# Sixty-four more bytes in each x and h tile of two fused MLPs

## The chip, the core and the metric

The kernel runs on one core of a Trainium2 chip. The metric is the device time of one execution in microseconds; the kernel before was run three times, and the median counts. One further execution was taken by the hardware profiler, and every row below is from it.

## The reference, cut to what matters

The program is an attention with mixed heads, followed by two MLPs on its 1792 x 768 output:

```
scores = einsum(q @ k.T / 8, w_pre) over heads;  attn = softmax(scores)
x = (einsum(attn, w_post) over heads) @ v          # 1792 tokens x 768
h = x @ moe_w_in      (768 -> 2048);  h = elu(h);      x = h @ moe_w_out   (2048 -> 768)
h = x @ moe2_w_in     (768 -> 2048);  h = relu(h)**2;  out = h @ moe2_w_out (2048 -> 768)
```

Inputs and outputs are float32. The MLP weights arrive in float64 and are turned into float32 on the chip.

## The kernel before, in words

The attention comes first and takes about 430 us. The MLPs fill the rest, in two halves of 896 tokens. Everything in them that goes through TensorE is split into a high part (rounded to the type float32r) and a low part (the rest, also float32r). A product is made of three matmuls that add into one PSUM bank: high by high, high by low and low by high (`three`, L582 to L586).

In a matmul one operand is loaded into the array beforehand (the stationary one, by an LDWEIGHTS row, engine PEld) and the other is streamed through it (the moving one, row MATMUL, engine PE). The trace names a matmul as output<-moving,stationary. In three of the four layers the weights are stationary and the activations move, transposed, in pieces of 448 tokens (a float32r row of 1792 bytes per partition):

- first layer of the first MLP: `xh` and `xl` move past `wh` and `wl` (`inner`, L588)
- second layer of the first MLP: `hh` and `hl` move past `wh` and `wl` (loop at L645)
- first layer of the second MLP: `xh` and `xl` again (`inner`)
- second layer of the second MLP: here `hh` and `hl` are stationary, 128 tokens at a time, and `wh` and `wl` move in pieces of 384 columns (loop at L662)

With 16 blocks of 128 hidden units, 6 blocks of 128 model units, 2 pieces of 448 tokens and 2 halves, each of the lines L584, L585 and L586 runs 768 times with x moving and 384 times with h moving, that is 3456 matmuls of 448 columns in the three lines together. With wh and wl moving there are 16 x 2 x 7 x 2 = 448 per line, 1344 in all.

The order of the work is fixed by the order of the code on each engine. For every unit of weights (128 rows by 384 or 512 columns) SP starts a load, ScalarE and VectorE turn it into float32 and split it into `wh` and `wl` (`Weights`), two units ahead of its use. Between these, ScalarE and VectorE apply the activation to a finished bank and split the result into `hh` and `hl` (L617 to L626) or `xh` and `xl` (L655, L656).

The tiles `xh`, `xl`, `hh` and `hl` are made by `two_parts` (L524). A tile is 64 bytes longer than its content (`2 * OFF` floats with OFF = 8), and its content begins at float `at`: 8 for x, 0 for the h of the first MLP, 8 for the h of the second. Tiles of a pool lie one behind the other in each partition, the high one first. With the pools as they stand, the high parts begin, where they move, at a multiple of 128 bytes, and the low parts 64 bytes past one.

Of the kernel before, what the change touches and what calls it, by code (L numbers as in the profile page):

```python
# [8 lines left out]
F32R = mybir.dt.float32r  # L9
# [14 lines left out]
OFF = 8  # L24
# [481 lines left out]
class Mlps:  # L506
# [17 lines left out]
    def two_parts(self, k, pool, name, at):  # L524

        n = k * 2 * S
        t = [pool.tile([128, n + 2 * OFF], F32R, name=f"{name}{a}", tag=f"{name}{a}") for a in "hl"]
        return [x[:, at : at + n].rearrange("p (k s) -> p k s", k=k) for x in t]


# [199 lines left out]
```

## Time and profile before

| | us |
|---|---|
| median of 3 runs (lowest to highest) | 1381.85 (1380.25 to 1382.3) |
| profiled execution, time | 1380.11 |
| its span, first to last instruction | 1378.3 |
| TensorE matmuls busy in the span | 1366.5 (99%) |
| VectorE busy | 859.0 (62%) |
| ScalarE busy | 669.5 (49%) |
| GpSimd busy | 263.4 (19%) |

Matmuls are pipelined: a row's duration reaches from the start of a matmul to its modelled end, and the next one begins long before that. What a stream of matmuls costs is therefore read from the distance between the starts of two that follow each other, not from the durations. The granted clock of TensorE, a column of the windows below, is a share of 2.4 GHz, at which 448 columns take 186.7 ns and 384 columns 160.0 ns.

### The profile page before, as it was taken

The page shows a single profiled execution, that of the slowest core. Times are in us where ns is not written, and L with a number is a line of the kernel's source. Part 1 is how long each engine was busy: PE and PEld are TensorE (multiplying, and loading weights), DVE is VectorE, ACT ScalarE, POOL GpSimd, SP SyncE. Part 2 cuts the span into 40 slices and gives each one's busy share as a digit, 9 for nine tenths or more (in the row PEclk, how much of TensorE's full clock was granted, in tenths as well). Part 3 has the DMA queues.
Part 4 walks back from the last instruction along what each step waited for, and adds up shares of the span by engine and source line. Part 5 has one row for each costly group of instructions (what it writes and reads, how often), then busy time and mean ns, then how long its engine had stood idle before and what let it go on. Part 6 is the DMA issues. An engine that isn't in the chain of part 4 may idle for free.

```text
span 1378.3 us, 24196 instructions
## 1 busy us (share of the span) xinstructions
PE 1366.5 (99%) x8908; PEld 1247.3 (90%) x8908; DVE 859.0 (62%) x1928; ACT 669.5 (49%) x1504; POOL 263.4 (19%) x245
## 2 busy tenths in 40 slices
PE   7999999999999999999999999999999999999998
PEld 4888888888888999999999999999999999999998
DVE  6877778777886999866699996634442113443121
ACT  5776767776766667422355543235541113333111
POOL 3765655674656000000000000000000000000000
PEclk9999999999999999999999999999999999999999
DMA  5624633733644655545454576431121111111131
GB/s 155 203 106 134 197 106 126 210 119 114 201 139 129 200 167 175 185 156 171 128 164 158 173 251 194 156 103 58 54 77 54 47 46 46 58 52 58 41 109 40
DMA packets 104810, 174.40 MB, mean 127 GB/s; under 512 B 22675, under 2 KB 82163, under 8 KB 104691
## 3 DMA queue, kind: packets, MB, share of 16 engines
q1 hardware_dynamic: 104691, 172.85, 39.7%
q8 instruction: 70, 1.15, 0.3%
q14 instruction: 49, 0.40, 0.1%
HBM read 97.93 MB, written 36.18 MB: 97 GB/s over the span
## 4 chain that ended last, share of the span: by engine, by line
PE 97%; DVE 1%; ACT 0%; issue 0%; DMA 0%; POOL 0%; SPq 0%; ACTq 0%; DVEq 0%; POOLq 0%
PE ps_post L221 12%; PE ps_qk L585 11%; PE ps_qk L586 11%; PE ps_qk L584 11%; PE ps_qk L246 6%; PE ps_mix L585 6%; PE ps_post L585 6%; PE ps_post L586 6%; PE ps_mix L586 6%; PE ps_mix L584 6%; PE ps_post L584 6%; PE ps_qk L163 4%; PE ps_mix L192 3%; PE ps_mix L190 3%; PE ps_mix L191 3%
## 5 line engine op out<-in xcount | busy, mean ns | idle before, releaser
L472 ACT CAST wh<-wf 128x384 fp32r<-128x384 f32 (+1 forms) x240 | 126.7, 532 | 272.8 <-DVE wf L458 115.6
L473 DVE TENSOR_TENSOR wl<-wf,wh 128x384 fp32r<-128x384 f32 (+1 forms) x238 | 137.3, 580 | 158.2 <-ACT wh L472 157.2
L184 POOL TENSOR_TENSOR gl<-graw,gh 120x448 fp32r<-120x448 f32 x178 | 201.5, 1154 | 145.7 <-ACT gh L179 139.7
L221 PEld LDWEIGHTS ps_post<-wg,ex 120*112 120x112 f32 x1440 | 156.9, 177 | 20.6 <-DVE tot L205 7.5
L221 PE MATMUL ps_post<-wg,ex 120*112 120x120 f32 x1440 | 173.3, 273 | 0.0
L199 ACT ACTIVATE ex<-ps_mix,nmax 120x448 f32<-120x448 f32 x180 | 113.3, 636 | 113.0 <-DVE nmax L197 109.6
L585 PE MATMUL ps_qk<-xl,wh 128*128 128x448 f32 x384 | 141.0, 367 | 0.0
L586 PE MATMUL ps_qk<-xh,wl 128*128 128x448 f32 x384 | 140.6, 366 | 0.0
L584 PE MATMUL ps_qk<-xh,wh 128*128 128x448 f32 x384 | 139.4, 363 | 0.0
L197 DVE TENSOR_REDUCE nmax<-ps_mix 120x1 f32<-120x448 f32 x180 | 109.7, 622 | 41.8 <-PE ps_mix L192 41.4
L228 DVE COPY at<-ps_post 112x480 f32<-112x480 f32 x162 | 105.4, 650 | 10.0 <-PE ps_post L221 10.0
L179 ACT CAST gh<-graw 120x448 fp32r<-120x448 f32 x180 | 95.2, 593 | 0.6 <-DMA graw<-sc 0.5
L622 DVE TENSOR_TENSOR tmp<-tmp 128x448 f32<-128x448 f32 x64 | 39.9, 623 | 73.7 <-ACT tmp L621 73.7
L166 ACT COPY sc<-ps_qk 120x448 f32<-120x448 f32 x178 | 82.0, 557 | 7.2 <-PE ps_qk L163 7.0
L246 PEld LDWEIGHTS ps_qk<-at,v 112*64 112x64 f32 x1536 | 73.8, 137 | 11.3 <-ACT gh L179 6.2
L246 PE MATMUL ps_qk<-at,v 112*64 112x110 f32 (+2 forms) x1536 | 81.8, 262 | 0.0
L584 PEld LDWEIGHTS ps_qk<-xh,wh 128*128 128x128 f32 x384 | 72.3, 188 | 6.4
L585 PEld LDWEIGHTS ps_qk<-xl,wh 128*128 128x128 f32 x384 | 72.0, 187 | 6.3
L586 PEld LDWEIGHTS ps_qk<-xh,wl 128*128 128x128 f32 x384 | 72.0, 187 | 5.3
L434 ACT ACTIVATE wf<-wd 128x384 f32<-128x384 f32 (+1 forms) x120 | 69.5, 579 | 13.4 <-DMA wd<-w1i 7.9
L585 PE MATMUL ps_qk<-wl,hh 128*128 128x384 f32 x224 | 75.3, 336 | 0.0
L584 PE MATMUL ps_qk<-wh,hh 128*128 128x384 f32 x224 | 75.3, 336 | 0.0
(139 smaller groups left out, 3151.0 us busy)
## 6 DMA issues: line engine op xcount, KB each, us to landing
graw<-sc SPq DMA_DIRECT2D x180, 210.0 KB
wd<-w1i SPq DMA_DIRECT2D x32, 384.0 KB
wd<-w1o SPq DMA_DIRECT2D x24, 512.0 KB
wd<-w2i SPq DMA_DIRECT2D x32, 384.0 KB
wd<-w2o SPq DMA_DIRECT2D x32, 384.0 KB
w1if<-wf SPq DMA_DIRECT2D x32, 192.0 KB
w1of<-wf SPq DMA_DIRECT2D x24, 256.0 KB
w2if<-wf SPq DMA_DIRECT2D x32, 192.0 KB
```

The costliest lines, as they stand in the source:

```text
L179: nc.scalar.copy(hi, graw[t])
L184: engine.tensor_tensor(lo, graw.pop(t), parts[t][0].bitcast(F32), ALU.subtract)
L197: nc.vector.tensor_reduce(nmax, p, AX.X, ALU.max, negate=True)
L199: nc.scalar.activation(e[-1], p, AF.Exp, bias=nmax, scale=1.0, accum_out=tot[:, t % 2 : t % 2 + 1])
L221: nc.tensor.matmul(p[:, c, :], e[:, c * NJ : (c + 1) * NJ], w, start=True, stop=True)
L228: nc.vector.tensor_copy(o, p)
L246: nc.tensor.matmul(p[64 * a : 64 * a + 64, k, :w], vt[b, i][:, jc, g * D : (g + 1) * D], at[n][:, jc, 6 * i + g, :w], start=(jc == 0), sto ...
L472: nc.scalar.copy(hi, f)
L473: (engine or nc.vector).tensor_tensor(lo, f, hi.bitcast(F32), ALU.subtract)
L584: mm(p, wh, xh, start=first, stop=False)
L585: mm(p, wh, xl, start=False, stop=False)
L586: mm(p, wl, xh, start=False, stop=last)
```

## The change

Each tile of `two_parts` is given 128 bytes beyond its content, where it had 64:

```diff
     def two_parts(self, k, pool, name, at):
 
         n = k * 2 * S
-        t = [pool.tile([128, n + 2 * OFF], F32R, name=f"{name}{a}", tag=f"{name}{a}") for a in "hl"]
+        t = [pool.tile([128, n + 4 * OFF], F32R, name=f"{name}{a}", tag=f"{name}{a}") for a in "hl"]
         return [x[:, at : at + n].rearrange("p (k s) -> p k s", k=k) for x in t]
```

No instruction is added, removed or moved on any engine. What changes is where tiles lie in a partition. The contents are 21,504 bytes for x and 57,344 for h, both multiples of 128, as the pieces of 1792 bytes in them are. This is the first byte of the content, with its remainder by 128:

| content | before | after |
|---|---|---|
| xh, moving | 186,240 (0) | 186,112 (0) |
| xl, moving | 207,808 (64) | 207,744 (0) |
| hh of the first MLP, moving | 16,512 (0) | 16,512 (0) |
| hl of the first MLP, moving | 73,920 (64) | 73,984 (0) |
| hh of the second MLP, stationary | 16,544 (32) | 16,544 (32) |
| hl of the second MLP, stationary | 73,952 (96) | 74,016 (32) |
| wh, wl of three layers, stationary | (96) | 128 bytes lower (96) |
| wh, wl of the last layer, moving | (0) | 128 bytes lower (0) |

The pools of tmp, wd and wf lie 128 bytes lower too. The attention's tiles stay where they are; in its L190 to L192 the moving tiles gh and gl all begin at remainder 64.

## Rows read from the trace of the kernel before

**Rows 1.** The page: busy time of each engine; the chain that ended last, by engine.
```profile
PE 1366.5 (99%) x8908; PEld 1247.3 (90%) x8908; DVE 859.0 (62%) x1928; ACT 669.5 (49%) x1504; POOL 263.4 (19%) x245
...
PE 97%; DVE 1%; ACT 0%; issue 0%; DMA 0%; POOL 0%; SPq 0%; ACTq 0%; DVEq 0%; POOLq 0%
```

**Rows 2.** Groups by line, PE; names, tile, count | busy us, mean ns | idle us before.
```profile
L585 PE MATMUL ps_qk<-xl,wh 128*128 128x448 f32 x384 | 141.0, 367 | 0.0
L586 PE MATMUL ps_qk<-xh,wl 128*128 128x448 f32 x384 | 140.6, 366 | 0.0
L584 PE MATMUL ps_qk<-xh,wh 128*128 128x448 f32 x384 | 139.4, 363 | 0.0
...
L585 PE MATMUL ps_qk<-hl,wh 128*128 128x448 f32 x192 | 70.5, 367 | 0.0
```

**Rows 3.** Timeline, PE, 600 to 640: start us, duration us; first and last of 197.
```profile
599.81 0.37 PE L586 MATMUL ps_post<-hh,wl 128*128 128x448 f32 x1
...
639.66 0.36 PE L584 MATMUL ps_mix<-hh,wh 128*128 128x448 f32 x1
```

**Rows 4.** Timeline, PE, 1200 to 1240: first and last of 197 rows.
```profile
1199.83 0.37 PE L585 MATMUL ps_qk<-xl,wh 128*128 128x448 f32 x1
...
1239.68 0.37 PE L586 MATMUL ps_post<-xh,wl 128*128 128x448 f32 x1
```

**Rows 5.** Timeline, PE, 830 to 864: first and last of 197 rows.
```profile
829.69 0.34 PE L586 MATMUL ps_post<-wh,hl 128*128 128x384 f32 x1
...
863.66 0.34 PE L584 MATMUL ps_mix<-wh,hh 128*128 128x384 f32 x1
```

**Rows 6.** Timeline, PE, 500 to 501.3: seven matmuls in a row.
```profile
499.97 0.36 PE L584 MATMUL ps_post<-xh,wh 128*128 128x448 f32 x1
500.17 0.37 PE L585 MATMUL ps_post<-xl,wh 128*128 128x448 f32 x1
500.38 0.37 PE L586 MATMUL ps_post<-xh,wl 128*128 128x448 f32 x1
500.58 0.36 PE L584 MATMUL ps_post<-xh,wh 128*128 128x448 f32 x1
500.78 0.37 PE L585 MATMUL ps_post<-xl,wh 128*128 128x448 f32 x1
500.99 0.37 PE L586 MATMUL ps_post<-xh,wl 128*128 128x448 f32 x1
501.19 0.36 PE L584 MATMUL ps_mix<-xh,wh 128*128 128x448 f32 x1
```

**Rows 7.** Timeline, PE, 136.5 to 138: the attention's mixing matmuls, moving operands at 64.
```profile
136.71 0.36 PE L191 MATMUL ps_mix<-gh,pre_h 120*120 120x448 f32 x1
136.90 0.36 PE L192 MATMUL ps_mix<-gl,pre_h 120*120 120x448 f32 x1
137.10 0.36 PE L190 MATMUL ps_mix<-gh,pre_l 120*120 120x448 f32 x1
137.30 0.36 PE L191 MATMUL ps_mix<-gh,pre_h 120*120 120x448 f32 x1
137.50 0.37 PE L192 MATMUL ps_mix<-gl,pre_h 120*120 120x448 f32 x1
```

**Rows 8.** Timeline, PE, 93.9 to 95.3: first and last of five such matmuls.
```profile
94.05 0.36 PE L191 MATMUL ps_mix<-gh,pre_h 120*120 120x448 f32 x1
...
94.86 0.37 PE L192 MATMUL ps_mix<-gl,pre_h 120*120 120x448 f32 x1
```

**Rows 9.** Windows: from:to, us, busy (count) by engine, granted clock, DMA, GB/s.
```profile
450.00:550.00 100.00, 100.00 (x494) 92.30 (x493) 91.93 (x194) 68.72 (x138) 0.00 (x0) 1.00 0.56 179
560.00:660.00 100.00, 100.00 (x494) 92.30 (x493) 66.52 (x118) 30.16 (x53) 0.00 (x0) 1.00 0.51 162
800.00:890.00 90.00, 90.00 (x521) 90.00 (x520) 67.69 (x145) 31.85 (x65) 0.00 (x0) 1.00 0.64 205
1145.00:1245.00 100.00, 100.00 (x494) 92.30 (x493) 43.61 (x81) 38.58 (x82) 0.00 (x0) 1.00 0.18 53
```

**Rows 10.** Groups by line, VectorE, 430 to 1378: the writers of hl and xl.
```profile
L626 DVE TENSOR_TENSOR hl<-tmp,hh 128x448 fp32r<-128x448 f32 x128 | 74.1, 619 | 1.7 <-DMA xd<-xs 1.3
...
L656 DVE TENSOR_TENSOR xl<-ps_qk,xh 128x448 fp32r<-128x448 f32 x12 | 7.5, 624 | 40.3 <-ACT xh L655 40.3
```

## The prediction

> **What bounds the kernel now.** The first view to read is the page's busy line and its chain by engine [rows 1]: TensorE's matmuls are busy 99% of the span, and 97% of the chain that ended last is PE. So no wait of TensorE is to be removed, and a change counts if, and only if, it alters the rate at which matmuls follow one another. The second view, the groups by line, says that the matmuls of the MLPs sat idle for 0.0 us [rows 2]. Their durations there (363, 367 and 366 ns) overlap and are no cost; the column to read is the start, in the timeline.
>
> The timeline gives the rate. With h moving, the 197 rows from 599.81 to 639.66 make 196 steps of 39.85 / 196 = 203.3 ns [rows 3]. With x moving, in a late stage, it is again 39.85 / 196 = 203.3 ns [rows 4]. With the weights moving, in pieces of 384, it is 33.97 / 196 = 173.3 ns [rows 5]. The windows say what else goes on: VectorE is busy 92, 67 and 44 of 100 us and DMA 56, 51 and 18%, while TensorE starts the same 494 matmuls in each, at a granted clock of 1.00, the 2.4 GHz level [rows 9]. So the rate depends on no other engine and on no transfer; it is TensorE's own.
>
> At 2.4 GHz, 384 columns take 160.0 ns and 448 take 186.7. So a 384-column matmul costs 13.3 ns beyond its columns (173.3 - 160.0, 32 cycles), and a 448-column one 16.7 ns (203.3 - 186.7, 40 cycles). Both come each with one weight load of 128 columns. What differs, beside the length, is where the moving operands begin: all three of a group at a multiple of 128 bytes in the 384 case, and at 0, 64, 0 past one in the 448 case. The 3.3 ns between the two surpluses are what the change may win.
>
> **The change part by part.** (a) Nothing is issued more or less, and no queue is passed, so no instruction has to be priced; only places of tiles differ. (b) xl and hl move from remainder 64 to 0. They are one moving operand in three. The trace of before shows no 448-column stream with all three at 0, so its price is bounded. From below: the length may carry the 3.3 ns, and then it is 203.3 ns, nothing gained; an actual loss is the last rival. From above: the surplus of the aligned 384-column stream, 13.3 ns, as both load 128 weight columns per matmul; then it is 186.7 + 13.3 = 200.0 ns [rows 5]. Between the two lie the attention's mixing matmuls, 448 columns of the same type, all at remainder 64, with loads of 120 columns. Four steps there take 137.50 - 136.71 = 0.79 us in one place, 198 ns each [rows 7], and 94.86 - 94.05 = 0.81 us, 203 ns each, in another [rows 8]. A long row of 448 columns can thus run at about 200 ns when all its operands begin alike, which speaks against blaming the length. I take 200.0 ns, as the row nearest in type, weights and alignment is the 384-column one, and keep 203.3 for the range.
>
> The sum: 768 + 384 = 1152 matmuls in each of three lines, 3456 in all (the 384 rows of xl into ps_qk, two of four banks, are half of the 768 [rows 2]). 3456 x 3.33 ns = 11.5 us off 3456 x 203.3 ns = 703 us. The gain is not on xl's own matmul alone: the small differences inside a group (0.20 to 0.21 us from row to row [rows 6]) don't put it there, so the sum takes the whole group of three, 10 ns in 610.
>
> The Trainium skill has a rule that speaks against this. The profile shows 203.3 ns where the operands begin at 0, 64, 0 [rows 3]; the page SBUF — State Buffer, section "Door 1: The DMA port swizzle", says that consecutive accesses to one 16-byte line run at full bandwidth and that each crossing into a new line pays. By it, a start at 64 past 128 cuts no line and the alignment would be free, so the sum would be 0; this is the third case below. No run here shows that line.
>
> The skill's page TensorE: Matmul & The Clock Gate, section "Back-to-back issue gap", gives columns / 2.4 + 2.5 ns for a warm gap, an estimate of 189.2 ns for 448. The trace's 203.3 and 173.3 are both above what it gives, so the measured floor of the 384 case is used.
>
> (c) hl of the second MLP is stationary; its loads go from remainder 96 to 32. hh is loaded from 32 already, in the same stream with the same 0.0 us idle and 173.3 ns [rows 5]. I take 0 for it and bound it in the last rival; a gain is excluded, as I see it, since hh and hl share one rate now. (d) VectorE writes hl and xl, 619 and 624 ns each [rows 10], at another remainder. Should these become a few per cent slower or faster, 128 x 619 ns lies beside TensorE: 1% is 0.8 us on an engine with 8 of 100 us free in the fullest window. So 0. (e) wd, wf and tmp move by 128 bytes; transfers fill 56% of the DMA engines at most and hold nobody up. So 0.
>
> What comes late next: in the first layers VectorE works 91.93 us while TensorE takes 100 [rows 9]. At the new rate the same work stands beside 98.4 us, 93.4%. The cover holds on the mean; weights are made two units ahead, which bridges single late ones. If it failed, the loss would be limited to these layers: the first halves of the two first layers hold 1152 matmuls, 3.8 us of the gain.
>
> The profiled execution: 1380.11 - 11.5 = 1368.6 us. The median of the runs shown lies 1.74 above that execution, so 1370.4 us are predicted for the median.
>
> **The rivals.** A difference under 0.2%, 2.8 us, is about what a measurement of this kernel can't tell from no change.
>
> 1. Full gain, forecast: 200.0 ns, 1370.4 us; with rounding and 1 us of ripple at VectorE's pace, 1369 to 1372.5.
> 2. Part of it. Either equal remainders help only as far as the mixing rows show on the mean of their two places, (198 + 203) / 2 = 200 to 201.5 ns with the rounding of 10 ns in a timeline's start; at 201.5 it is 3456 x 1.8 = 6.2 us, 1375.6. Or VectorE takes back the 3.8 us above, 1374.2. For it: the two places differ though their operands begin alike. Against it: the even 173.3 ns of the 384 stream. 1372.5 to 1379.
> 3. No change: the 40 cycles belong to a piece of 448 columns, whatever its start. For it: a step after xh, which begins at 0, is no shorter by more than 0.01 us than one after xl [rows 6], so the cost isn't seen on the operand at 64. Against it: rows 7. 1381.9 us.
> 4. Slower: the load of the next weights and the moving operand get in each other's way where both begin at certain remainders. In before, xh with wl has a load behind it and a step of 0.20 to 0.21, no better than xl [rows 6]. The price: xl and hl become like xh with wl, at worst half the timeline's resolution, 5 ns, on 1152 matmuls, 5.8 us, if being at 64 has until now kept them out of the way; and hl's loads at 32, one for each of 448 groups of 384 columns, at most the same surplus of 3.3 ns, 1.5 us. Together 7.3 us, 1389.1. It decides against the change as soon as the collision costs more than 2.4 ns per low part. Against it: the 384 stream, where all begin at 0 past loads from 32 and 96, is the better one of the two. It would stand at 1384.7 to 1389.1.
>
> That the change doesn't do what it says is excluded by the addresses: 207,744 and 73,984 are 1623 and 578 times 128.
>
> **How the numbers follow.** I give the full gain 0.45, a part of it 0.20, no change 0.24 and slower 0.11. The first two are faster by over 0.2%: 0.65. The forecast is the likeliest case, 1370.4 us. The range for 8 in 10 starts 1.9 us below it, at 1368.5, for a surplus a little under 13.3 ns (0.5 ns less is 1.9 us), takes in the partial cases and most of the unchanged one, and ends at 1382.7.
>
> **What would show it.** In the profile after: 197 rows of timeline in a 448-column stretch should take 196 x 0.2000 = 39.2 us instead of 39.85, for h and for x alike; a window of 100 us should hold 502 matmuls instead of 494; the 384-column stretch should stay at 173.3 ns; VectorE in the first stretch should stand near 93%. It is wrong if the 448-column rate stays at 203.3 (case 3), if only x or only h changes, if TensorE shows idle time in the first layers (the second half of case 2), or if the 384-column stretch slows (case 4).

## The result, and the profile after

The changed kernel is slower: 1388.63 us (median of 4, 1387.04 to 1388.68) against 1381.88 for the kernel before on the same chip; ratio 1.0053, 95% interval 1.0042 to 1.0065. The forecast was 1370.4.

The page of the changed kernel, busy time by engine, and its chain by engine, against [rows 1]:

```profile
PE 1372.6 (99%) x8908; PEld 1250.9 (90%) x8908; DVE 859.4 (62%) x1928; ACT 669.5 (48%) x1504; POOL 263.3 (19%) x245
...
PE 97%; DVE 1%; ACT 1%; issue 0%; DMA 0%; POOL 0%; SPq 0%; ACTq 0%; DVEq 0%; POOLq 0%
```

All the other engines do what they did; TensorE's matmuls (PE) alone are busy 6.1 us longer, with their weight loads (PEld) beside them. The same windows as in [rows 9], of the changed kernel:

```profile
450.00:550.00 100.00, 100.00 (x491) 91.98 (x490) 91.52 (x194) 67.68 (x137) 0.00 (x0) 1.00 0.56 178
560.00:660.00 100.00, 100.00 (x491) 91.72 (x490) 66.02 (x117) 30.50 (x54) 0.00 (x0) 1.00 0.49 160
800.00:890.00 90.00, 90.00 (x514) 90.00 (x513) 67.66 (x145) 32.83 (x66) 0.00 (x0) 1.00 0.66 210
1145.00:1245.00 100.00, 100.00 (x491) 92.00 (x490) 43.89 (x81) 38.20 (x81) 0.00 (x0) 1.00 0.18 53
```

A window of 100 us holds 491 matmuls where it held 494, and 90 us of the 384-column stage hold 514 where they held 521. The granted clock is 1.00 in all of them, and VectorE's load falls from 92 to 44 us as before, with the same 491 matmuls beside it: the loss is in TensorE's own rate again, now also in the last layer. The exact rate comes from the timeline. This is the changed kernel from 600 to 640 (first and last of 197 rows, against [rows 3]) and from 830 to 864 (195 rows, against [rows 5]):

```profile
599.84 0.37 PE L584 MATMUL ps_post<-hh,wh 128*128 128x448 f32 x1
...
639.91 0.37 PE L585 MATMUL ps_post<-hl,wh 128*128 128x448 f32 x1
...
829.82 0.34 PE L584 MATMUL ps_post<-wh,hh 128*128 128x384 f32 x1
...
863.87 0.34 PE L586 MATMUL ps_post<-wh,hl 128*128 128x384 f32 x1
```

40.07 / 196 = 204.4 ns for 448 columns (203.3 before), 34.05 / 194 = 175.5 ns for 384 (173.3 before). Over the long stretches of the trace the rates are steady enough to count in cycles of 2.4 GHz: 490.67 instead of 488.00, and 421.33 instead of 416.00. With 3456 x 1.11 ns = 3.8 us and 1344 x 2.22 ns = 3.0 us that makes 6.8 us, the whole difference (1388.63 - 1381.88 = 6.75).

### The profile page after: what moved, and what is told of

Read it like the earlier page. It is cut to its first block, busy times and chain, and to the rows that moved or that the text cites. A ratio compares the mean times of both kernels' runs of the same rounds, so it can differ in the third digit from the quotient of the medians.

```text
span 1385.3 us, 24196 instructions
## 1 busy us (share of the span) xinstructions
PE 1372.6 (99%) x8908; PEld 1250.9 (90%) x8908; DVE 859.4 (62%) x1928; ACT 669.5 (48%) x1504; POOL 263.3 (19%) x245
## 4 chain that ended last, share of the span: by engine, by line
PE 97%; DVE 1%; ACT 1%; issue 0%; DMA 0%; POOL 0%; SPq 0%; ACTq 0%; DVEq 0%; POOLq 0%
PE ps_post L221 11%; PE ps_qk L585 11%; PE ps_qk L584 11%; PE ps_qk L586 11%; PE ps_qk L246 6%; PE ps_mix L585 6%; PE ps_mix L584 6%; PE ps_post L585 6%; PE ps_post L584 6%; PE ps_post L586 6%; PE ps_mix L586 6%; PE ps_qk L163 4%; PE ps_mix L192 2%; PE ps_mix L190 2%; PE ps_mix L191 2%
## 5 line engine op out<-in xcount | busy, mean ns | idle before, releaser
L586 PE MATMUL ps_qk<-wh,hl 128*128 128x384 f32 x224 | 76.5, 341 | 0.0
```

The source lines that it names most:

```text
L586: mm(p, wl, xh, start=False, stop=last)
```

## The experiments

The floor of a matmul is taken below as its columns + 32 cycles (480 for 448 columns, 416 for 384), and the surplus is what it takes beyond. Before, 448 columns have 8.0 cycles of surplus and 384 none; after, 10.67 and 5.33. Distance means the first byte of a stationary operand less the first byte of a moving one, as a remainder by 256.

**The change in parts.** Three runs: the x tiles alone, the h tiles alone, and neither but the same displacement of x, the weights and the other tiles behind them.

```diff
# e1_x_only
+        t = [pool.tile([128, n + (4 if name == "x" else 2) * OFF], ...
# e2_h_only
+        t = [pool.tile([128, n + (4 if name == "h" else 2) * OFF], ...
# e3_displaced_only
+        t = [pool.tile([128, n + (6 if name + a == "xl" else 2) * OFF], ...
```

Expected of the x tiles alone:

> Only the x tiles get the 64 extra bytes; the h tiles are as before. xl moves from remainder 64 to 0; xh, tmp and the weight tiles lie 128 bytes lower; hl is as before. Three theories for the 6.8 us lost. Pair theory: what costs is where the stationary operand that is being loaded lies against the operand that moves meanwhile, by 128 bytes; then the x stages take 204.4 ns a matmul as in the changed kernel, the h stage stays at 203.3 and the 384-column stage at 173.3, so 2304 x 1.1 ns, about 2.5 us over before (1384.4). Start theory: a low part that starts at 0 as the high part does costs by itself; the same numbers here. Displacement theory: the 128 bytes by which weights and x are displaced (remainder by 256) cost, and the start of the low part nothing; then all stages are as in the changed kernel, 204.4 and 175.6 ns, about 1388.6.

Expected of the h tiles alone:

> Only the h tiles get the 64 extra bytes; x, tmp and the weight tiles lie where they lay before. hl moves to remainder 0 in the first MLP and is stationary at 32 instead of 96 in the second. Pair theory: x stages 203.3 ns, h stage 204.4, and the 384-column stage 175.6, as there only the place of the stationary hl against the moving weights has changed: 1152 x 1.1 ns + 1344 x 2.2 ns, about 4.3 us over before (1386.2). Start theory: h stage 204.4, 384-column stage 173.3, as nothing that moves there has another start: about 1.3 us over (1383.2). Displacement theory: all as before, 1381.9.

Expected of the displacement alone:

> The low x tile gets 128 bytes more behind its content and nothing else is changed: x, tmp and the weight tiles lie 128 bytes lower as in the changed kernel, and the low parts still begin at remainder 64. Pair theory by 128 bytes and start theory: all stages as before, 203.3 and 173.3 ns, 1381.9. Displacement theory: all stages as in the changed kernel, 204.4 and 175.6 ns, about 1388.6.

Measured: ratios to the kernel before of 1.0047 (95% interval 1.0032 to 1.0062), 1.0034 (1.0021 to 1.0047) and 1.0029 (1.0018 to 1.004). Windows of the displacement run, one in an h stage, one in an x stage, one in the 384-column stage:

```profile
560.00:660.00 100.00, 100.00 (x491) 91.97 (x490) 66.68 (x119) 30.93 (x54) 0.00 (x0) 1.00 0.51 163
690.00:790.00 100.00, 100.00 (x494) 92.39 (x493) 90.93 (x191) 52.59 (x110) 0.00 (x0) 1.00 0.52 161
800.00:890.00 90.00, 90.00 (x514) 90.00 (x514) 67.61 (x145) 32.85 (x66) 0.00 (x0) 1.00 0.66 212
```

With every low part left at remainder 64, the h stage and the 384-column stage are as slow as in the changed kernel (491 and 514), and the x stage is as fast as before (494). So the start of the low parts is not needed for most of the loss. x and the weights were displaced together there, and keep their rate; h was not, and loses. The h stage and the 384-column stage of the run with h alone:

```profile
560.00:660.00 100.00, 100.00 (x491) 91.98 (x490) 66.05 (x117) 30.14 (x53) 0.00 (x0) 1.00 0.49 162
...
800.00:890.00 90.00, 90.00 (x514) 90.00 (x513) 67.71 (x145) 32.37 (x65) 0.00 (x0) 1.00 0.64 205
```

Here the weights lie as before, and moving hl alone costs the same: in the last layer, where hl is only loaded, 514 instead of 521. None of the three theories as I had put them fits all three runs. What fits is the pair theory with 256 bytes in place of 128: each stage keeps its rate as long as the distances between its operands stay the same by 256. In the list below, m is the moving operand and s the stationary one, and the distances are those for high moving and low moving (448 columns) or hh and hl loaded (384):

```
                     x: m 448 columns        h: m 448 columns        last layer, 384 columns
before               224, 160 -> 203.3 ns    224, 160 -> 203.3 ns    32,  96 -> 173.3 ns
e3 displaced only    224, 160 -> 203.3        96,  32 -> 204.4      160, 224 -> 175.6
e2 h only            224, 160 -> 203.3       224,  96 -> 204.4       32, 160 -> 175.6
e1 x only            224,  96 -> 204.4        96,  32 -> 204.4      160, 224 -> 175.6
after                224,  96 -> 204.4        96, 224 -> 204.4      160,  32 -> 175.6
```

**The grid.** A kernel that only streams matmuls, to measure the disputed cost by itself. Its core:

```python
for n, mh, ml, sh, sl in combos():          # starts in bytes past a multiple of 256
    for group in range(8):
        mm(p, wh, xh); mm(p, wh, xl); mm(p, wl, xh)
```

Expected of the grid:

> No attention and no MLP is computed: this kernel only measures. It streams 238 sequences of 24 matmuls each, in the MLPs' groups of three (high by high, high weights by low, low weights by high), from one tile, with the operands' starts set to chosen remainders by 256 bytes, and writes zeros. Read is the distance between starts, in cycles of 2.4 GHz, over the floor of columns + 32. Pair theory: the rate depends on the stationary start less the moving start, and the configurations of the two kernels come out as there: 0 for 384 columns with moving 0 and stationary 32 and 96, 16 cycles per group of three with stationary 32 and 32, 24 for 448 columns with moving 0, 64, 0 past stationary 96, 32 with moving 0, 0, 0. Start theory: the rate depends on the moving starts alone, one value per row of moving starts whatever the stationary ones. Displacement theory: moving both by 128 against each other changes the rate.

Measured, for 448 columns with all moving parts at one start and all stationary ones at another, 64 sequences: the surplus goes with the difference of the two, by 256 bytes, with the same values along each diagonal of the table but for three sequences: 0 gave about 20 in place of 48 where both begin at 0 or both at 32, and 224 gave 48 in place of 32 once. Per group of three, in cycles:

```
distance            0    32    64    96   128   160   192   224
surplus of three   48    32    16     0    29    38     0    32
```

The mixed sequences with the distances of the real stages gave 31 to 32 for the changed kernel's 448 columns (32 in the kernel) and 18 for its 384 columns (16); for the kernel before 28 (24) and 1 (0). Streams of 24 are short, so a few cycles of their start remain in these numbers; from the tenth matmul on they are 32, 16, 24 and 0, what the two kernels have. The pair theory holds, by 256 bytes. The start theory falls, since the rate changes along every row of moving starts. So does the idea that the parts of a group add up: with the changed kernel's distances of 96, 224, 96 the even streams of the table would give (0 + 32 + 0) / 3 = 11, and it is 32.

**A kernel by that rule, and two that contradict it.** High and low parts alike by 256, weights 96 past them:

```diff
# b1_all_96 (OFF no longer used; b2_all_0: tmp as before, 40 for 16; b3_256_room: the change with 8 * OFF)
-        t = [pool.tile([128, n + 2 * OFF], F32R, ...) for a in "hl"]
+        t = [pool.tile([128, n + (24 if name + a == "xl" else 0)], F32R, ...) for a in "hl"]
-        return self.tp.tile([128, S], F32, name="tmp", bufs=5)
+        return self.tp.tile([128, S + 8], F32, name="tmp", bufs=5)[:, :S]
-        at = OFF * self.units[i][4]
+        at = 16 * self.units[i][4]
```

The starts of x and h (`at`) are 0 in the first two. In the run at 0 the stationary parts of the three layers lie 0 past the moving ones; its last layer is at 96, as in the run at 96.

Expected at 96:

> A kernel laid out by the rule of the grid run: high and low parts start at the same remainder by 256 bytes (128), the stationary operands 96 past the moving ones by 256, in all four layers (xl has 96 bytes more room and xh, hh, hl none, contents begin at 0; tmp is 8 floats longer; the weights that move begin 64 bytes into their tiles). Distance rule (the rate of an even stream depends on stationary start less moving start, by 256, and 96 is free of surplus): 448 columns at 200.0 ns, 384 at 173.3: 3456 x 3.33 = 11.5 us under before, ratio 0.9917. If the grid run's rates don't carry over to the whole kernel, about before.

Expected at 0:

> The same layout without the longer tmp tiles, so that x, h and the weights that lie stationary all start at 128 by 256, distance 0; in the last layer the weights move from 160 bytes into their tiles, distance 96 as in the run beside. Both parts begin alike here and at a multiple of 128 bytes, which is what the change was to bring about. Distance rule: 448 columns take 16 cycles more than the floor, 206.7 ns, and 384 stay at 173.3: 3456 x 3.33 = 11.5 us over before, ratio 1.0083. Start theory (low and high parts that begin alike at a multiple of 128 run at the floor): 200.0 ns, 11.5 us under before, ratio 0.9917.

Expected of 256 bytes of room:

> One number of the change is different: 8 * OFF floats of room (256 bytes) instead of 4 * OFF (128), so that the low parts begin at the same remainder by 256 as the high ones; x then moves from 0 with weights loaded from 224, h from 128 with weights from 224, and in the last layer the weights move from 0 with both h parts loaded from 160. Distance rule with the grid's even streams: x stages (distance 224) 32 cycles per group of three over the floor, 204.4 ns; h stages (distance 96) at the floor, 200.0 ns; 384 columns (distance 160) 24 to 38 cycles per group, 176.7 to 178.6 ns; in all 2304 x 1.1 - 1152 x 3.3 + 1344 x (3.3 to 5.3) ns, 3.2 to 5.9 us over before, ratio 1.0023 to 1.0043. Start theory: 200.0 and 173.3 ns everywhere, 11.5 us under before.

Measured: 0.9949 (0.9935 to 0.9963), 1.0033 (1.002 to 1.0045), 1.0073 (1.0059 to 1.0087); the distance rule had asked for 0.9917, 1.0083 and 1.0023 to 1.0043, so all three missed it. At 96 the h stage holds 502 matmuls in 100 us, 200.0 ns, the floor; but the last layer fell to 512 in 90 us (176.7 ns), which I had put at the floor:

```profile
800.00:890.00 90.00, 90.00 (x512) 90.00 (x511) 65.69 (x140) 30.02 (x61) 0.00 (x0) 1.00 0.61 196
560.00:660.00 100.00, 100.00 (x502) 93.84 (x501) 67.55 (x120) 30.43 (x55) 0.00 (x0) 1.00 0.51 166
```

The other two hold a surprise. Both run each h stage twice, once per half of the tokens, with the same tiles. Windows of the run at 0 (two h stages), and then of the run with 256 bytes of room (two h stages at distance 96):

```profile
560.00:660.00 100.00, 100.00 (x495) 92.67 (x494) 66.83 (x119) 30.17 (x53) 0.00 (x0) 1.00 0.50 163
1030.00:1130.00 100.00, 100.00 (x485) 90.83 (x485) 19.42 (x31) 17.24 (x31) 0.00 (x0) 1.00 0.18 54
```

```profile
560.00:660.00 100.00, 100.00 (x486) 90.48 (x484) 65.62 (x116) 30.38 (x54) 0.00 (x0) 1.00 0.49 163
1030.00:1130.00 100.00, 100.00 (x501) 93.78 (x500) 22.15 (x36) 21.08 (x38) 0.00 (x0) 1.00 0.17 53
```

At distance 0 the first stage takes 202.7 ns and the second 206.7; at 96 the first takes 206.7 and the second 200.0. At 0 the slower stage is the one where VectorE has least to do, 19 of 100 us, so a busy VectorE is not the cause. The last layer shows the same across two kernels: with moving and stationary parts at the same starts by 256, distance 96, it runs at 176.7 ns in the run at 96 above and at 173.3 in the run at 0:

```profile
800.00:890.00 90.00, 90.00 (x521) 90.00 (x520) 67.70 (x146) 31.89 (x64) 0.00 (x0) 1.00 0.64 206
```

A distance allows more than one steady rate. It is not chance from one execution to the next: the five executions of the run at 0 lie within 1.1 us and the four of the run with 256 bytes of room within 1.8, and one h stage of 576 matmuls at its other rate would be 2.3 us in the first and 3.8 in the second. The start theory, which is what the prediction rested on, asked for 200.0 ns in both kernels; both are slower than before.

**Distance in finer steps, and the entry.** Two more measuring kernels: streams of 48 at one distance in steps of 16 bytes, and pairs of streams, the first (36 matmuls) at one of eight distances, the second (48) at the target. Each distance and each pair ran once, in a fixed order.

Expected of the finer steps:

> Again only a measuring kernel: neither attention nor MLPs are computed. Streams of 48 matmuls with all moving parts at 0 and all stationary ones at the same distance, in steps of 16 bytes, over 768 bytes for 448 columns and over 256 for 256, 384 and 512. Distance rule: the surplus over columns + 32 repeats every 256 bytes, with 0 at 96 and 192 and 16 cycles per matmul at 0, and the same for the four lengths if it is the load's own. If the load meets the moving operand at a place that depends on the length, the free distances differ between the lengths. If lines of 128 bytes decide, it repeats every 128.

Expected of the pairs:

> A measuring kernel, nothing of the reference is computed: 88 pairs of streams without a gap, 36 matmuls of 448 columns at one distance, then 48 of 448 or of 384 columns at another. If the distance alone sets the rate, every target distance shows one rate whatever went before: 448 columns 6.4 or 16 cycles over columns + 32 at 0, 10.7 at 32, 0 at 96 and 192, 10.7 or 16 at 224; 384 columns 0 at 32, 48, 64, 96 and 192. If the entry decides too, as the two halves of the run with distance 0 suggest (202.7 and 206.7 ns at one distance), some target distances show two rates or more, with the stream before as the only difference, and 96 shows 16 cycles in some rows for 448 and 8 in some for 384.

Measured by distance, over 768 bytes: the pattern repeats every 256 bytes, not every 128, to within 0.2 cycles per matmul. For 448 columns 0 is reached at 96 and 192 alone of the 16 steps, and the worst steps, 16 and 224, have 16 cycles; for 384 columns ten of the sixteen steps are free (0 to 64, 96, 112, 176, 192, 240); for 512 columns 0, 16 and 240. So the free distances do depend on the length; a distance with more than one rate shows here the one that this order gives it. This is the timeline of the stream at 96 (the ends of 40 rows), and of the one at 224 (of 38 rows):

```profile
99.94 0.36 PE L71 MATMUL ps<-work 128*128 128x448 f32 x1
100.14 0.36 PE L69 MATMUL ps<-work 128*128 128x448 f32 x1
...
107.55 0.36 PE L70 MATMUL ps<-work 128*128 128x448 f32 x1
107.75 0.36 PE L71 MATMUL ps<-work 128*128 128x448 f32 x1
```

```profile
178.21 0.37 PE L69 MATMUL ps<-work 128*128 128x448 f32 x1
...
185.86 0.37 PE L70 MATMUL ps<-work 128*128 128x448 f32 x1
```

The first is 7.81 / 39 = 200 ns from start to start, the second 7.65 / 37 = 207 ns.

Measured by entry, surplus in cycles per matmul of the second stream, by the distance of the first (0, 32, ... 224):

```
448 columns at   0    6.4   6.1   6.4   6.1   6.3   6.6  16.0  16.0
448 columns at  32   10.7  10.7  10.6  10.6  10.7   7.9  10.7  10.7
448 columns at  96    0     0     0     0     0     0     0    16.0
448 columns at 192    0     0     0     0     0     0     0     0
448 columns at 224   16.0  16.0   0    16.0  16.0  10.7  16.0  16.0
384 columns at   0, 32, 48 and 192: 0 in all eight
384 columns at  64    0     7.9   7.9   3.3   3.1   8.1   7.9   3.3
384 columns at  96    0     7.8   0     0     0     0     0     0
```

The target at 96 after a stream at 192, and the same target after a stream at 224, windows of 7.6 us of that kernel:

```profile
402.20:409.80 7.60, 7.60 (x40) 7.13 (x39) 0.00 (x0) 0.00 (x0) 1.00 0.00 0
419.20:426.80 7.60, 7.60 (x39) 6.87 (x38) 0.00 (x0) 0.00 (x0) 1.00 0.01 2
```

Nothing but TensorE works there, and the second streams are the same code with the same starts; what ran before them differs. It is what the first h stage of the run with 256 bytes of room showed, at 96 behind an x stage at 224, with 16 cycles of surplus. So the entry decides too, but the distance of the stream before does not say how. The second h stage of that run also came at 96 behind an x stage at 224, and had none. The x stages before the two differ in their rate, 204.4 and 206.7 ns:

```profile
450.00:550.00 100.00, 100.00 (x491) 91.57 (x490) 91.75 (x194) 67.99 (x137) 0.00 (x0) 1.00 0.57 179
920.00:1020.00 100.00, 100.00 (x485) 90.97 (x485) 44.30 (x82) 54.66 (x110) 0.00 (x0) 1.00 0.19 55
```

The rate of the stream before doesn't say it either: in the pairs the stream at 224 ran at 206.7 ns and 16 cycles followed, in the kernel 206.7 was followed by none. And 384 columns at 96 behind 448 at 96 had no surplus in the pairs, but 8 cycles in the last layer of the run at 96. What it is in the entry that decides stays open. The targets that showed one rate after all entries tried are 192 for 448 columns, and 0, 32, 48 and 192 for 384.

**The last layer at a distance that showed one rate.** Two versions of the run at 96:

```diff
# b4_384_at_32                                # b5_384_as_before: the same, and
-        at = 16 * self.units[i][4]           # hl of the second MLP 64 bytes further
+        at = 32 * self.units[i][4]
```

Expected at 32:

> As the run with distance 96 in all layers, but in the last layer the weights move from 128 bytes into their tiles, so that the stationary hh and hl lie 32 past them instead of 96. Distance rule with entry (a distance allows one or more steady rates, and what ran before decides which): at 32 the grids show 173.3 ns for 384 columns in every stream, so 1344 x 3.33 = 4.5 us under the run with 96, ratio to before 0.9917. If the 176.7 ns of that run come from what runs before the stage and hold at any distance, as there, 0.9949.

Expected with the old distances:

> As the run beside, with 64 bytes more room in hl and the low h of the second MLP 64 bytes further, so that in the last layer hh lies 32 and hl 96 past the moving weights, the distances that the kernel before has there (32, 96, 32 at 173.3 ns). Distance rule with entry: 173.3 ns, as before and as beside, ratio 0.9917. If the entry decides alone: 176.7 ns, 0.9949.

Measured: 1368.88 us, ratio 0.9915 (0.9902 to 0.9929), and 1369.65 us, 0.992 (0.9906 to 0.9933). The same windows once more, of the version at 32:

```profile
450.00:550.00 100.00, 100.00 (x502) 93.84 (x501) 93.50 (x198) 69.12 (x139) 0.00 (x0) 1.00 0.58 184
560.00:660.00 100.00, 100.00 (x502) 93.84 (x501) 67.62 (x120) 30.44 (x54) 0.00 (x0) 1.00 0.50 166
800.00:890.00 90.00, 90.00 (x521) 90.00 (x520) 66.31 (x142) 30.88 (x62) 0.00 (x0) 1.00 0.62 198
1145.00:1245.00 100.00, 100.00 (x502) 93.84 (x501) 45.64 (x84) 39.70 (x84) 0.00 (x0) 1.00 0.19 55
```

All four stages stand at the floor, 502 in 100 us and 521 in 90; with the old distances of 32 and 96 the last layer holds 521 too, so what runs before it does not decide alone. The version at 32 beats both kernels, by 3456 x 3.33 ns = 11.5 us against the kernel before (0.0085 x 1380.54 = 11.7 measured).

## Why the prediction was wrong

*What bounds the kernel, and that its rate is TensorE's own.* Right: in every run of the whole kernel the loss or gain is, within its interval, the number of matmuls times the change of their spacing. The size of the gain was right as well: 200.0 ns for 448 columns, taken over from the 13.3 ns of the 384-column rows, is what the version at 32 runs at, 11.7 us under the kernel before. The way to it was wrong.

*(b), the place of xl and hl.* This is the step that failed. It took the start of the moving operands, by 128 bytes, for what sets the surplus, and the 384-column stream for a proof of it. The runs show the distance between the stationary and the moving operand, by 256 bytes. In the changed kernel the low part has come to lie 128 bytes from the high one by 256, at distances of 96 and 224, with a surplus of 32 cycles per group of three instead of 24: 3.8 us lost where 11.5 were forecast as gain. The 384-column stream was at the floor because of its distances (32, 96) and its length, not because its moving operands begin at a multiple of 128: the run with h alone leaves those where they were and has 175.6 ns. The test that this reading asked for, both parts alike at a multiple of 128, is the run at 0: slower than before.

*(c), hl as a stationary operand, and the displaced tiles, put at 0.* Both were wrong. (e) names only wd, wf and tmp; that xh and the weights wh and wl also come to lie 128 bytes lower has no term in the sum, since their remainder by 128 stays, and this is the larger omission. That displacement alone costs 0.29%: 1152 x 1.11 ns in the h stages and 1344 x 2.22 ns in the last layer are 4.3 us. Moving hl alone gives the last layer the same 2.22 ns, 3.0 us. The two don't add up: with both, it is still 175.6 ns.

*(d), VectorE, and what comes late next.* Right. At 200.0 ns, in the version at 32, VectorE stands at 93.50 of 100 us, where 93.4% was forecast, and no surplus appears in that stage; the cover holds.

*The rivals.* The last one, the load and the moving operand in each other's way where both begin at certain remainders, had the right pair of operands, and its sign, a slower 384-column stretch, came. Its sum, 2.8 to 7.3 us, holds the 6.8 measured, but by luck and not by its terms: 5.8 at most for 448 columns and 1.5 at most for 384 were written, and 3.8 and 3.0 came. A row that spoke for it was in hand: the mixing matmuls, whose moving operands all begin alike, ran at 198 and at 203 ns [rows 7, 8]. The prediction used that for a partial gain; it can also be read as a sign that something else than the moving start decides, though five matmuls in a row show little. The partial and the unchanged case fell with (b). A slip without weight: at the lower end of the range, 0.5 ns on 3456 matmuls is 1.7 us, not 1.9.

*The rule weighed against the change.* The Trainium skill's page SBUF — State Buffer, section "Door 1: The DMA port swizzle", read as the prediction reads it (a start moved by whole lines of 16 bytes costs nothing), would have given 0 for hl moved by 64 bytes. The run with h alone shows 0.34%, so the measurement decides against that reading. The Trainium skill's page TensorE: Matmul & The Clock Gate, section "Step-by-step: what each phase is for", says that two independent read ports feed the moving operand and the weight load. Here the spacing depends on the starts of the two together, by up to 6.7 ns at 448 columns; where in their way the two meet is not shown.

## What to carry to other kernels

Where TensorE is the bound, count the spacing of matmuls in cycles from the timeline, and compare it with the best spacing seen at the same load; a steady surplus of some cycles can be a matter of where tiles lie. Then lay out stationary against moving operands on purpose, by their distance; where high and low parts begin alike there is one distance to choose instead of two. Padding one tile displaces every tile behind it and changes distances that were good. A short measuring kernel that streams all candidate layouts in one run replaces many guesses, but its rates must be seen again in the whole kernel, since a distance can have more than one.

## What was not expected of the hardware

- With float32r operands and a load of 128 columns beside each matmul, the spacing is a steady 480 cycles for 448 columns at best, and up to 496, by the distance between the two operands, with a period of 256 bytes over the 768 tried. A shift of 4 bytes can matter: 10.6 cycles at a distance of 4, none at 8, each seen in one stream.
- The same stream at the same distance can settle at two rates (0 or 16 cycles at 96, 6.4 or 16 at 0), and stays there for a whole stage of 576 matmuls. What ran before has a part in it.
- Streams of 256 columns went below their columns + 32, to 272 cycles at distances of 64 and 192, so 32 is not a floor for every length.

What sets the period of 256 bytes and which rate a stream falls into is not shown by these runs, nor why three unequal distances don't give the mean of the even streams, nor whether a moving operand counts against the stationary one in use or against the one loaded behind it: wh and wl begin alike in these kernels.
